# A float32 chain of decayed attention and two gated layers on one core: decay tables from prefix scans, first loads in another order, a new written order

## The chip, the cores and the metric

The kernel runs on one core of one Trainium2 chip. The metric is the device time of one execution in microseconds (us); the time given for a kernel is the median of its runs. A core has a matrix engine (TensorE, PE in the profile; PEld is its loading of weights), a vector engine (VectorE, DVE), an activation engine (ScalarE, ACT), a general engine (GpSimd, POOL) and a sync engine (SyncE, SP). Here SP issues most transfers (DMAs) and ACT a few. Every engine works through its own list of instructions in order; between engines they wait on semaphores.

## The reference

Three stages, all float32. `q`, `k`, `v` are 2 x 8 x 768 x 64 (batches, heads, tokens, channels), `lam` holds one decay factor a head, near 0.98.

```
intra = (q k^T * Dmask) v              # in a block; Dmask[i, j] = lam^(i-j) for i >= j, else 0
inter = (q * lam^(pos+1)) state        # what the blocks before left
state = lam^block * state + (k * lam^(block-1-pos))^T v
x  = attention output as 1536 x 512
xn = x / sqrt(mean(x*x) + 1e-6) * rms_g
x  = (silu(xn w_gate) * (xn w_val)) w_out      # 512 -> 1536 -> 512
x  = ((x w_a) * (x w_b)) w_out2                # 512 -> 1536 -> 512
```

## The kernel before, in words

Attention is cut into chunks of 128 tokens, six for each of the two batches. The weights arrive as 8-byte doubles and are turned into float32 on the chip: ACT copies two bytes of each (`conv_copy`, L275), DVE does the rest in seven steps (`conv_op`, L288 to L312). The two layers' matrix products take float32 operands split into a rounded high part (ACT, L325) and a low remainder (DVE, L330), three products a pair (L543, L544, L547, L599; L746 where the second layer and part of the first share block products).

The whole order of the program is written out by hand in `PROGRAM`, a list of words. A word is a step and its arguments; each step issues its instructions on its engines, and each engine keeps the order of the list. The words that matter here:

- `A.b.c.p`: SP loads two parts (or one) of batch b's chunk c, from part p on. Parts 0 and 1 are q and k by channels, 2 and 3 are v and k by tokens. `L.b.c` loads a whole later chunk. `l.n` loads the n-th third of the weights (512 KB, into one of three buffers `stage`).
- `S.b.c` scores (PE, L373, 16 passes), `am.b.c.r` the mask (DVE, L384): scores times the decay table `dt` for the even (r = 0) or odd heads. `X.b.c` masked scores times v (L423). `kd` decays k (ACT, eight small multiplications by the last column of `dt`, L366), `U` makes k^T v from it (L393), `I` is the inter-chunk product (L408) of q decayed by `qd` (DVE, L361, with the table `p1`, a part of `dec`).
- `xs`, `xd`: the attention output's high part (ACT, L456) and low part (DVE, L462, four instructions of 128 x 128). `sq`, `rh`, `rd`, `R`, `ms`: the mean square.
- `c.i.p` and `k.i.op.p` the conversion of weight block i, `hi.g.p` and `lo.g.p` its split, `G.g` and `V.g` the gate and value products (12 passes of 512 columns each on PE). `G.0` is the first of them and needs the attention output of chunks 0 and 1 of both batches.
- `W.n.1`: n dummy matmuls that nobody reads (`keep_warm`).

The tables are `dt`, 128 x 2 x 4 x 128 (for each head a triangle of powers), and `p1`, 128 x 4 x 128 (lam^(i+1)). Before the change they are made in three steps. DVE writes zeros, a one and the powers of `lam` into `ext` (8 rows of 256) by seven doublings (L858). ACT stores `ext` to DRAM (word `Z`). ACT then reads it back, each partition from an address shifted by one element (words `D.0` for `dt` and `D.1` for `p1`, two transfers each).

DMAs take eight completion semaphores in turn (`DMAHW0` to `DMAHW7`, SP's and ACT's together): where one is taken again, its issue waits until the transfer that had it has landed.

Of the kernel before, what the change touches and what calls it, by code (L numbers as in the profile page):

```python
# [44 lines left out]
def beside(i, t):  # L45
# [865 lines left out]
```

## Time and profile before

| | |
|---|---|
| time, median of 3 runs | 648.26 us (647.26 to 648.41) |
| time of the profiled execution | 647.11 us |
| its span, first to last instruction | 645.2 us |
| PE busy in the span | 626.1 us (97%) |
| DVE busy | 519.6 us (81%) |
| ACT busy | 374.4 us (58%) |
| POOL busy | 6.4 us (1%) |

The span is what the trace shows; 1.91 us of the execution lie around it. A busy share over the whole span says which engine is loaded, not what a stretch waits for; the rows further down take the span in stretches.

### The profile page before, as it was taken

To read this page: it belongs to the slowest core of one execution; us is meant where nothing else is said; L and a number is where in the kernel's file an instruction comes from. 1 tells how busy PE (TensorE), PEld (TensorE's weight loads), DVE (VectorE), ACT (ScalarE), POOL (GpSimd) and SP (SyncE) were. 2 spreads that over 40 slices of the span, in tenths; PEclk is the share of its full clock that TensorE was granted. 3 is DMA by queue.
4 is the path that set the end of the run, shared out by engine and by line. 5 is a ranking of instruction groups with operands and counts; after the bars stand their busy time and mean duration, and the time that the engine had idled before them with its cause. 6 is when DMAs were issued, how large, how long until landed. Compare 5 with 4: busy or idle time off the path is not lost.

```text
span 645.2 us, 8760 instructions
## 1 busy us (share of the span) xinstructions
PE 626.1 (97%) x3238; PEld 513.1 (80%) x3238; DVE 519.6 (81%) x965; ACT 374.4 (58%) x704; POOL 6.4 (1%) x15
## 2 busy tenths in 40 slices
PE   6689999999999999999999999999999999999997
PEld 3667888888888888888887888888888888888886
DVE  3678987888999889777989999999979854765673
ACT  2679877564558755455756655675567533443451
POOL 0000000000000000000000000000000000000000
PEclk8789999999999999999999999999999999999999
DMA  8826896432311230223002243121223000100011
GB/s 278 297 95 229 254 326 231 169 99 67 130 50 65 99 132 6 93 98 99 1 1 75 92 128 131 34 95 36 66 67 98 1 1 0 67 0 2 0 66 65
DMA packets 20394, 61.91 MB, mean 96 GB/s; under 512 B 2296, under 2 KB 3840, under 8 KB 19328
## 3 DMA queue, kind: packets, MB, share of 16 engines
q1 hardware_dynamic: 17872, 54.27, 25.2%
q10 hardware_dynamic: 2480, 7.09, 3.3%
q8 instruction: 25, 0.41, 0.3%
q14 instruction: 17, 0.14, 0.1%
HBM read 55.84 MB, written 5.51 MB: 95 GB/s over the span
## 4 chain that ended last, share of the span: by engine, by line
PE 92%; DVE 3%; DMA 2%; ACT 1%; issue 0%; ACTq 0%
PE acc L599 29%; PE at L746 17%; PE gv L746 13%; PE gv L543 6%; PE gv L544 6%; PE gv L547 6%; PE at L543 3%; PE at L544 3%; PE at L547 3%; PE at L373 2%; DMA dt<-ext_d 1%; PE at L408 1%; PE at L423 1%; DVE sums L611 1%; DMA ext_d<-nrm 1%; PE acc L423 1%
## 5 line engine op out<-in xcount | busy, mean ns | idle before, releaser
L275 ACT COPY hh<-stage 128x1024 uint8<-128x1024 uint8 x72 | 74.5, 1044 | 22.2 <-DMA stage<-w_dram 9.0
L325 ACT CAST whi<-w 128x512 fp32r<-128x512 f32 (+1 forms) x102 | 57.6, 576 | 30.0 <-PE acc L599 12.1
L543 PE MATMUL gv<-xhi,whi 128*128 128x512 f32 x160 | 64.6, 403 | 0.0
L544 PE MATMUL gv<-xlo,whi 128*128 128x512 f32 x160 | 63.2, 395 | 0.0
L330 DVE TENSOR_TENSOR wlo<-w,whi 128x512 fp32r<-128x512 f32 (+1 forms) x90 | 55.5, 622 | 8.8 <-ACT whi L325 8.7
L325 ACT CAST whi<-o 128x512 fp32r<-128x512 f32 x72 | 43.8, 620 | 18.0 <-PE acc L599 6.6
L330 DVE TENSOR_TENSOR wlo<-o,whi 128x512 fp32r<-128x512 f32 x66 | 44.9, 685 | 5.8 <-ACT whi L325 5.8
L746 PE MATMUL at<-T,whi 128*128 128x512 f32 x172 | 46.0, 389 | 0.0
L599 PE MATMUL acc<-hhi,whi 128*128 128x512 f32 x144 | 43.9, 395 | 0.1
L599 PE MATMUL acc<-hlo,whi 128*128 128x512 f32 x144 | 43.8, 390 | 0.0
L547 PE MATMUL gv<-xhi,wlo 128*128 128x512 f32 x160 | 43.2, 392 | 0.0
L599 PE MATMUL acc<-whi,hlo 128*128 128x512 f32 x144 | 43.0, 389 | 0.0
L599 PE MATMUL acc<-hhi,wlo 128*128 128x512 f32 x144 | 43.0, 390 | 0.0
L599 PE MATMUL acc<-whi,hhi 128*128 128x512 f32 x144 | 41.7, 390 | 0.0
L599 PE MATMUL acc<-wlo,hhi 128*128 128x512 f32 x144 | 41.4, 389 | 0.0
L330 DVE TENSOR_TENSOR wlo<-wsum,whi 128x512 fp32r<-128x512 f32 x42 | 28.8, 686 | 13.9 <-ACT whi L325 13.8
L746 PEld LDWEIGHTS at<-T,whi 128*128 128x128 f32 x172 | 32.2, 188 | 6.8 <-issue 0.2
L543 PEld LDWEIGHTS gv<-xhi,whi 128*128 128x128 f32 x160 | 30.3, 190 | 6.9 <-issue 0.5
L547 PEld LDWEIGHTS gv<-xhi,wlo 128*128 128x128 f32 x160 | 30.5, 190 | 6.5
L544 PEld LDWEIGHTS gv<-xlo,whi 128*128 128x128 f32 x160 | 30.5, 191 | 6.1 <-DVE xlo L527 0.2
L325 ACT CAST whi<-wsum 128x512 fp32r<-128x512 f32 x42 | 26.0, 621 | 13.5 <-DVE wsum L715 8.6
L746 PE MATMUL at<-xhi,whi 128*128 128x512 f32 x86 | 33.7, 391 | 0.0
(169 smaller groups left out, 1412.2 us busy)
## 6 DMA issues: line engine op xcount, KB each, us to landing
stage<-w_dram SPq DMA_DIRECT2D x72, 512.0 KB, 3.5
att<-att_dram ACTq DMA_DIRECT2D x6, 1024.0 KB, 6.3
wlo<-wlo_d SPq DMA_DIRECT2D x18, 256.0 KB, 3.7
att<-att_dram SPq DMA_DIRECT2D x6, 512.0 KB, 6.1
out_dram<-sums SPq DMA_DIRECT2D x12, 256.0 KB, 2.1
wlo_d<-wlo SPq DMA_DIRECT2D x9, 256.0 KB, 5.3
att<-att_dram SPq DMA_DIRECT2D x2, 1024.0 KB, 9.0
att<-att_dram SPq DMA_DIRECT2D x4, 256.0 KB, 6.9
```

Source lines behind the costliest of these rows:

```text
L275: nc.scalar.copy(hh_t[i][:, into].bitcast(U8).rearrange("p (n e) -> p n e", e=2), st.rearrange("p (n e) -> p n e", e=8)[:, :, 3:5],)
L325: nc.scalar.copy(whi[key], src)
L330: nc.vector.tensor_sub(wlo[key], src, whi[key].bitcast(F32))
L373: nc.tensor.matmul(ps[r][:, a * C : (a + 1) * C], lhsT=t[r * D : (r + 1) * D, 1, a * C : (a + 1) * C], rhs=t[r * D : (r + 1) * D, 0, a * C ...
L408: nc.tensor.matmul(px_t[b, c][r * D : (r + 1) * D, a * C : (a + 1) * C], lhsT=st_t[b][r * D : (r + 1) * D, a, :], rhs=kq_t[b, c][r * D : ( ...
L423: nc.tensor.matmul(px_t[b, c][r * D : (r + 1) * D, a * C : (a + 1) * C], lhsT=att_t[b, c][:, 2, h * D : (h + 1) * D], rhs=a_t[b, c][:, r, ...
L543: nc.tensor.matmul(ps, lhsT=w, rhs=xhi[t][:, k, :], start=k == 0, stop=False)
L544: nc.tensor.matmul(ps, lhsT=w, rhs=xlo[t][:, k, :], start=False, stop=False)
L547: nc.tensor.matmul(ps, lhsT=w, rhs=xhi[t][:, k, :], start=False, stop=k == KD - 1)
L599: nc.tensor.matmul(acc[j], lhsT=lhsT, rhs=rhs, start=first and n == 0, stop=last and n == 2)
L611: nc.vector.tensor_add(sums[t][:, j, :], sums[t][:, j, :], acc[j])
L746: nc.tensor.matmul(ps, lhsT=w[:, k * 128 : (k + 1) * 128], rhs=x[:, k, :], start=first and n == 0, stop=n == len(todo) - 1, skip_group_che ...
```

## The change

The tables no longer go by way of DRAM. `lam` is loaded into all 128 partitions at once (`lam_all`, 128 x 8). GpSimd writes an antidiagonal of ones (`anti`). VectorE makes each head's table with one prefix scan along 128 columns: eight scans for `dt`, four for `p1`. Word `D.r` is now the scans of the even or odd heads, `Z` those of `p1`. The seven doublings, the store and the four transfers back are gone; some constants are set by DVE instead of POOL.

```
-        nc.sync.dma_start(out=lam8, in_=lam)
+        nc.sync.dma_start(out=lam_all, in_=bass.AP(lam.tensor, lam.offset, [[0, 128], [1, H]]))
         nc.vector.memset(warm, 0.0)
-        nc.vector.memset(ext[:, 0:127], 0.0)
-        nc.vector.memset(ext[:, 127:128], 1.0)
-        nc.gpsimd.memset(ones, 1.0)
-        nc.gpsimd.memset(mhalf, -0.5)
-        nc.gpsimd.memset(ident, 1.0)
+        nc.vector.memset(mhalf, -0.5)
+        nc.vector.memset(ones, 1.0)
+        nc.vector.memset(ident, 1.0)
+        nc.gpsimd.affine_select(
+            out=anti, in_=ones, compare_op=ALU.is_equal, fill=0.0, base=1 - C,
+            pattern=[[1, 128]], channel_multiplier=1,
+        )
...
-        nc.vector.tensor_copy(ext[:, 128:129], lam8)
-        n = 1
-        while n < 128:
-            nc.vector.tensor_scalar_mul(
-                ext[:, 128 + n : 128 + 2 * n], ext[:, 128 : 128 + n], ext[:, 127 + n : 128 + n]
-            )
-            n *= 2
+        for r in range(2):
+            some = slice(r * D, (r + 1) * D)
+            nc.gpsimd.tensor_copy(lam_own[some], lam_all[some].rearrange("p (a r) -> p a r", r=2)[:, :, r])
...
+    def mask_table(r):
+
+        for a in range(NP):
+            h = 2 * a + r
+            nc.vector.tensor_tensor_scan(
+                out=dt[:, r, a, :], data0=lam_all[:, h : h + 1].to_broadcast([128, C]), data1=anti,
+                initial=0.0, op0=ALU.mult, op1=ALU.add,
+            )
+
+    def query_table():
+
+        for a in range(NP):
+            nc.vector.tensor_tensor_scan(
+                out=p1[:, a, :], data0=lam_own[:, a : a + 1].to_broadcast([128, C]), data1=ones,
+                initial=1.0, op0=ALU.mult, op1=ALU.mult,
+            )
```

`PROGRAM` is new from its first word up to word 992 of 2004; the words are the same ones, and from there on the order is the same. Its first line, before and now:

```
-    l.1 k.0.2.2 Z l.0 c.0.2 D.0 A.0.0.0 D.1 W.2.1 W.3.1 W.7.1 S.0.0 k.0.0.2 k.0.1.2 A.1.0.0 W.8.1 A.1.0.2 c.0.1 k.0.2.1
...
+    D.1 W.8.1 A.0.0.0 S.0.0 l.0 W.7.1 c.0.1 Z A.0.0.2 g D.0 am.0.0.1 A.1.0.0 k.0.0.1 am.0.0.0 l.1 k.0.1.1 X.0.0 kd.0.0
```

On DVE, at the start of the program, the difference of the two lists of instructions reads as follows (`-` before, `+` now; the scans print as SCALAR_TENSOR_TENSOR, `nrm` is the tile that holds `anti`, `w` a converted weight block, `am` a masked score).

```order
-L858 TENSOR_SCALAR nrm<-nrm 8x32
-L858 TENSOR_SCALAR nrm<-nrm 8x64
-L288 TENSOR_SCALAR w_122<-stage 128x512
+L847 MEMSET warm 128x256
+L848 MEMSET mhalf 128x2
+L849 MEMSET ones 128x128
+L850 MEMSET ident 128x128
+L795 SCALAR_TENSOR_TENSOR dt<-lam_all,nrm 128x128 x4
+L803 SCALAR_TENSOR_TENSOR dec<-lam_own,ones 128x128 x4
+L795 SCALAR_TENSOR_TENSOR dt<-lam_all,nrm 128x128 x4
+L384 TENSOR_TENSOR am<-at_129,dt 128x512
```

Twelve scans now stand ahead of the first mask, and the weight conversion that stood there comes after it.

On SP, the head of the queue before the change, with the semaphores that an issue waits for (`lam_84` is the factors, `att_0_131` batch 0's and `att_0_163` batch 1's chunk 0, `att_1` chunk 1, `g_sb` is `rms_g`):

```order
L843 DMA lam_84<-lam_dram 8x1
L249 DMA stage<-w_dram 128x4096 x2
L239 DMA att_0_131<-att_dram 128x1024
L239 DMA att_0_163<-att_dram 128x1024 x2
L239 DMA att_0_131<-att_dram 128x1024 [waits DMAHW2_49]
L239 DMA att_1_207<-att_dram 128x1024 [waits DMAHW4_49]
L239 DMA att_1_209<-att_dram 128x512 [waits DMAHW5_49]
L819 DMA g_sb<-gn_dram 128x4 [waits DMAHW6_49]
L239 DMA att_1_209<-att_dram 128x1024 [waits DMAHW7_49]
L239 DMA att_1_207<-att_dram 128x512 [waits DMAHW0_49]
L239 DMA att_1_207<-att_dram 128x512 [waits DMAHW1_49]
```

And now (`att_0_126` and `att_1_218` are batch 0, `att_0_161` and `att_1_229` batch 1):

```order
L846 DMA lam_all<-lam_dram 128x8
L239 DMA att_0_126<-att_dram 128x1024
L249 DMA stage<-w_dram 128x4096
L239 DMA att_0_126<-att_dram 128x1024
L822 DMA g_sb<-gn_dram 128x4
L239 DMA att_0_161<-att_dram 128x1024
L249 DMA stage<-w_dram 128x4096
L239 DMA att_0_161<-att_dram 128x1024
L239 DMA att_1_218<-att_dram 128x1024 [waits DMAHW0_49]
L239 DMA att_1_229<-att_dram 128x1024 [waits DMAHW1_49]
L239 DMA att_1_229<-att_dram 128x512 [waits DMAHW2_49]
L239 DMA att_1_218<-att_dram 128x512 [waits DMAHW3_49]
```

Batch 0's q and k are now the first large transfer, a weight load stands between the parts, and the eight semaphores are held by loads alone.

On ACT, the difference at the same place (`hh` are the copied bytes of the weights, `whi` a high part, `spare` and `kq` hold the decayed k):

```order
 L863 ACT_TABLE_LOAD
 L863 ACTIVATE mhalf<-mhalf 128x2
-L818 DMA ext_d<-nrm 8x256
-L275 COPY hh<-stage 128x1024
-L795 DMA dt<-ext_d 128x4x128 x2
-L800 DMA dec<-ext_d 64x4x128 x2
-L275 COPY hh<-stage 128x1024
-L325 CAST whi<-w_122 128x512
-L366 ACTIVATE spare<-att_0_163,dt 128x64 x8
-L366 ACTIVATE kq<-att_0_131,dt 128x64 x8
```

ACT's list loses the five issues of the tables' transfers; now the two rows at its head are followed by a weight copy and by the decay of batch 0's k.

## Rows read from the trace of the kernel before

**Rows 1.** Busy time by stretch: engines with instruction counts, granted clock, DMA share, GB/s.

```profile
core 0: us, PE busy (x) PEld busy (x) DVE busy (x) ACT busy (x) POOL busy (x), PEclk, DMA share, GB/s
0.00:17.34 17.34, 9.93 (x52) 4.91 (x52) 5.64 (x21) 4.17 (x6) 0.96 (x9) 0.90 0.85 269
17.34:41.40 24.06, 18.28 (x204) 16.00 (x205) 16.95 (x48) 16.23 (x52) 0.70 (x1) 0.79 0.67 233
41.40:86.70 45.30, 43.09 (x391) 35.97 (x390) 39.10 (x90) 39.65 (x109) 2.69 (x3) 0.96 0.70 229
86.70:360.00 273.30, 273.21 (x1356) 224.16 (x1357) 237.98 (x429) 167.33 (x295) 2.00 (x2) 1.00 0.29 96
360.00:645.20 285.20, 281.55 (x1240) 232.09 (x1238) 219.92 (x380) 146.97 (x247) 0.00 (x0) 1.00 0.16 52
```

**Rows 2.** The chain of waits, first microseconds: start, us, what.

```profile
0.79 1.32 DMA lam<-lam_dram
...
4.09 5.44 DMA ext_d<-nrm
...
10.03 8.59 DMA dt<-ext_d
```

**Rows 3.** Timeline of VectorE: start, us, operation, idle before and its releaser.

```profile
2.30 1.76 DVE L858 TENSOR_SCALAR nrm<-nrm 8x1 f32<-8x1 f32 x7
...
7.44 0.69 DVE L298 SCALAR_TENSOR_TENSOR w<-w,hh 128x512 f32<-128x512 uint32 x1
...
17.34 0.69 DVE L384 TENSOR_TENSOR am<-at,dt 128x512 f32<-128x512 f32 x1 [2.68 <-DMA dt<-ext_d]
```

**Rows 4.** Transfer queue of SP: who waited for whom, us in total, times, longest.

```profile
SPq L819 <- DMA dt<-ext_d: 6.9, 1, 6.9
```

**Rows 5.** Transfers: issue to landing of `g_sb` and `stage`; rates of two stretches.

```profile
g_sb<-gn_dram SPq DMA_DIRECT2D x1, 2.0 KB, 2.2
...
DMA to landing us min/median/max: 3.5/4.4/6.9
...
2.00:14.00 12.00, 9.17 (x51) 4.63 (x49) 4.65 (x16) 2.68 (x5) 0.10 (x1) 0.86 0.97 328
14.00:24.00 10.00, 5.29 (x52) 5.04 (x54) 5.86 (x13) 5.54 (x22) 0.00 (x0) 0.70 0.79 199
```

**Rows 6.** VectorE and GpSimd groups by shape: busy us, mean ns, idle before.

```profile
L384 DVE TENSOR_TENSOR am<-at,dt 128x512 f32<-128x512 f32 x8 | 5.4, 682 | 2.7 <-DMA dt<-ext_d 2.7
L462 DVE SCALAR_TENSOR_TENSOR xlo<-acc,g_sb,xhi 128x128 fp32r<-128x128 f32 x16 | 4.5, 344 | 3.4 <-ACT xhi L456 3.4
...
L288 DVE TENSOR_SCALAR w<-stage 128x512 uint32<-128x512 uint32 x6 | 2.5, 421 | 0.7 <-DMA stage<-w_dram 0.7
...
L305 DVE TENSOR_SCALAR t<-hh 128x512 uint16<-128x512 uint16 x5 | 1.4, 289 | 7.1 <-ACT hh L275 7.1
...
L494 POOL TENSOR_TENSOR rr<-ms,mhalf 128x2 f32<-128x2 f32 x6 | 5.4, 900 | 139.7 <-DVE ms L487 139.7
```

**Rows 7.** Timeline of TensorE: start, us, operation, idle before and its releaser.

```profile
8.21 2.08 PE L373 MATMUL at<-att 64*128 64x128 f32 x16 [2.47 <-DMA att<-att_dram]
10.22 2.36 PE L809 MATMUL gv<-warm 128*128 128x512 bf16 x8
...
20.58 0.44 PE L423 MATMUL acc<-am,att 128*64 128x128 f32 x1
...
31.32 1.68 PE L423 MATMUL acc<-am,att 128*64 128x128 f32 x16
...
41.40 0.47 PE L543 MATMUL gv<-xhi,whi 128*128 128x512 f32 x1
...
44.52 1.47 PE L547 MATMUL gv<-xhi,wlo 128*128 128x512 f32 x4
...
57.53 0.50 PE L543 MATMUL gv<-xhi,whi 128*128 128x512 f32 x1
...
59.48 1.07 PE L547 MATMUL gv<-xhi,wlo 128*128 128x512 f32 x4
```

More of the change, by code (lines that the diff above doesn't have):

```diff
@@ new lines @@
+    xs.0.0 sq.0.0 A.1.0.2 xd.0.0 S.1.0 U.0.0 A.0.1.0 c.0.2 kd.1.0 A.1.1.0 am.1.0.0 rh.0.0 W.3.1 am.1.0.1 k.0.2.1 rd.0.0
+    X.1.0 qd.0.1 R.0.0 sa.0.0 k.0.3.1 k.0.0.2 A.1.1.2 A.0.1.3 k.0.2.2 S.0.1 ms.0.0 A.0.1.2 U.1.0 l.4 qd.1.1 sq.1.0
+    xs.1.0 am.0.1.0 I.0.1 rh.1.0 am.0.1.1 S.1.1 xd.1.0 rd.1.0 am.1.1.0 kd.0.1 sa.1.0 sd.0.1 k.0.5.1 l.3 R.1.0 l.2 X.0.1
+    ms.1.0 c.1.1 k.0.1.2 am.1.1.1 U.0.1 sq.0.1 xs.0.1 k.1.2.1 I.1.1 X.1.1 rr.0 k.0.3.2 dg.0 rh.0.1 k.0.5.2 xs.1.1
+    A.1.1.3 L.0.2 N.0 rv.0 rd.0.1 k.0.6.1 xd.0.1 R.0.1 xd.1.1 c.1.0 sq.1.1 k.1.2.0 rh.1.1 ms.0.1 hi.0.0 rd.1.1 W.2.1
@@ new lines @@
+    kd.1.1 l.5 S.0.2 kd.0.2 k.1.0.0 R.1.1 L.1.2 lo.0.0 am.0.2.1 ms.1.1 k.1.1.0 qd.0.2 rr.1 dg.1 sa.0.1 G.0 N.1 rv.1
+    c.1.2 qd.1.2 am.0.2.0 k.2.2.0 k.1.0.1 k.1.3.0 k.1.0.2 I.0.2 X.0.2 sd.0.2 k.0.6.2 sq.0.2 xg.0.2 k.1.1.1 l.8 U.0.2
+    k.1.2.2 sa.0.2 k.1.1.2 rh.0.2 hi.0.1 L.0.3 k.1.3.2 U.1.1 S.1.2 k.1.3.1 lo.0.1 V.0 l.7 k.1.5.0 rd.0.2 k.1.5.1
+    am.1.2.1 ls.0.0 kd.1.2 sd.1.1 R.0.2 am.1.2.0 k.1.6.1 sa.1.1 c.2.0 U.1.2 ms.0.2 hi.1.0 gs.0 k.2.2.2 ls.0.1 l.6 I.1.2
+    si.0 X.1.2 qd.0.3 sd.1.2 lo.1.0 k.1.5.2 sq.1.2 mu.0 xg.1.2 k.1.6.2 sa.1.2 c.2.2 G.1 rh.1.2 c.2.1 hh.0 rd.1.2 R.1.2
@@ new lines @@
+    k.1.6.0 ms.1.2 hi.0.2 L.0.4 k.2.0 hi.1.1 kd.0.3 hl.0 S.0.3 am.0.3.1 I.0.3 rr.2 sd.0.3 am.0.3.0 l.9 k.2.1 hi.3.0
+    dg.2 k.2.3 lo.1.1 X.0.3 U.0.3 k.2.5 L.1.3 sq.0.3 k.2.2.1 xg.0.3 V.1 k.2.6 lo.0.2 N.2 nx.2.0 nx.2.2 O.0 rh.0.3
+    nx.2.1 l.10 nx.2.3 ls.1.0 rd.0.3 sa.0.3 hi.1.2 k.3.2.0 c.3.1 R.0.3 c.3.0 ms.0.3 qd.1.3 hi.2.0 l.11 S.1.3 hi.2.1
+    c.3.2 am.1.3.1 am.1.3.0 gs.1 I.1.3 k.3.2.1 kd.1.3 X.1.3 U.1.3 si.1 xg.1.3 l.12 lo.2.0 G.2 lo.1.2 sq.1.3 ls.1.1
+    k.3.2.2 rh.1.3 mu.1 rd.1.3 hi.4.0 hi.3.1 qd.0.4 lo.2.1 ls.2.0 l.13 ls.2.1 sd.1.3 R.1.3 hh.1 ms.1.3 rr.3 V.2 k.3.0
@@ new lines @@
+    gs.2 lr.4.0 xh.2.0 sa.1.3 kd.0.4 dg.3 hl.1 xl.2.0 N.3 L.1.4 lr.3.0 nx.3.3 O.1 hi.5.0 k.3.1 si.2 nx.3.0 nx.3.2
+    xh.2.1 xh.3.1 nx.3.1 xl.2.1 S.0.4 xl.3.1 xh.3.0 c.4.2 c.4.1 xl.3.0 lr.3.1 mu.2 c.4.0 k.3.3 am.0.4.1 hi.4.1 ls.0.2
+    G.3 ls.1.2 k.3.5 k.4.2.1 am.0.4.0 k.3.6 I.0.4 sd.0.4 U.0.4 si.3 X.0.4 sa.0.4 sq.0.4 hi.4.2 hh.2 l.16 V.3 k.4.2.0
+    hl.2 mu.3 hi.2.2 xg.0.4 kd.1.4 lo.2.2 c.5.2 rh.0.4 rd.0.4 S.1.4 G.4 hi.9.0 hh.3 hi.5.1 k.4.2.2 am.1.4.1 l.15 lr.5.0
+    lo.9.0 O.2 L.0.5 R.0.4 qd.1.4 lr.4.1 si.4 am.1.4.0 k.4.0 ms.0.4 V.4 c.5.1 I.1.4 k.5.2.2 lr.5.1 k.4.1 sd.1.4 E.2.0
@@ new lines @@
+    G.10 am.1.5.1 xh.4.0 lr.6.2 xl.4.1 gs.10 O.5 hi.7.1 rd.0.5 am.1.5.0 hh.9 k.6.3 k.6.5 l.22 R.0.5 k.6.6 G.11 V.10
+    ms.0.5 hl.9 k.8.2.0 hi.12.0 lr.7.2 c.7.2 gs.11 c.8.0 I.1.5 E.5.1 si.10 lo.12.0 mu.10 lo.9.2 X.1.5 E.5.3 hi.12.1
+    k.7.0.0 sq.1.5 E.5.0 rh.1.5 xg.1.5 G.12 E.5.2 lo.12.1 rd.1.5 k.7.2.0 xl.4.0 k.7.1.0 hh.10 R.1.5 ms.1.5 hi.11.1 rr.5
+    O.9 dg.5 si.11 lo.11.1 hi.10.2 hl.10 N.5 k.7.3.0 lo.10.2 k.7.5.0 l.24 nx.5.2 l.21 nx.5.0 nx.5.1 k.7.6.0 c.7.1 V.11
+    gs.12 mu.11 hh.11 nx.5.3 hi.6.1 xh.5.0 O.10 hl.11 hi.7.0 xh.5.1 lr.7.0 c.8.1 xl.5.0 k.7.0.2 tq.3.0 xl.5.1 tq.3.1
@@ new lines @@
+    k.7.3.1 P.3.5 ws.4.1 pa.3.1 ws.3.4 uh.3.2 P.3.6 ws.4.2 k.7.5.1 hi.7.2 P.4.2 ul.3.2 ps.3.6 P.3.7 hh.8 k.7.6.1 ps.3.5
+    hl.8 uh.4.1 l.28 k.8.2.2 sl.3.1 hi.8.2 k.8.0 l.26 ws.4.3 ws.4.4 P.3.3 pa.3.3 k.7.6.2 uh.4.2 ps.4.1 O.7 ps.3.7
+    ul.4.2 ul.3.3 ul.4.1 P.3.4 ws.5.3 pm.3.1 c.9.2 ws.5.1 uh.5.3 ph.3.1 lr.8.2 k.9.2.2 l.31 uh.5.0 pa.3.2 ws.5.2
+    k.9.2.1 P.4.5 k.9.2.0 uh.3.4 ps.4.5 O.8 k.8.1 E.8.0 pa.4.1 P.4.6 ul.5.0 uh.5.1 sl.3.2 k.8.3 pm.3.2 c.9.1 k.8.5
+    pl.3.1 ps.4.6 P.5.2 E.8.2 P.5.1 E.8.3 l.29 ps.5.1 ws.5.4 c.9.0 uh.4.3 ul.3.4 ul.5.1 P.4.3 pa.4.3 ws.6.1 P.4.7
@@ new lines @@
+    uh.4.4 ul.5.3 ul.4.4 ul.4.3 sl.4.1 P.5.6 l.30 ps.4.7 P.4.4 E.8.1 k.8.6 pa.5.1 P.5.5 uh.6.0 k.9.0 sl.4.2 Q.3.1.0.9
+    uh.5.2 ul.5.2 pa.4.2 Q.3.1.9.12 ws.6.2 ps.5.5 pm.4.1 sl.5.1 ps.5.6 ul.6.0 P.5.3 c.10.0 ph.4.1 pm.4.2 P.5.7 k.9.1
+    P.6.2 k.9.3 ws.6.4 c.10.1 pl.4.1 ps.5.7 P.6.1 c.10.2 Q.4.1.0.9 uh.6.1 Q.4.1.9.12 ws.6.3 pa.5.3 k.10.2.2 ps.6.1
+    k.9.5 k.10.0 hi.13.0 uh.5.4 ul.6.1 pa.6.1 k.9.6 sl.6.1 P.6.6 sl.5.2 k.10.2.0 ws.7.1 hi.14.1 uh.6.2 l.34 ps.6.6
+    k.10.2.1 P.6.5 P.5.4 k.10.1 lo.14.1 pm.5.1 ul.5.4 pa.5.2 ul.6.2 V.14 uh.6.3 pm.5.2 ps.6.5 k.11.2.2 k.10.3 P.6.7
@@ new lines @@
+    ph.5.1 P.6.3 ul.6.3 ps.6.7 lo.13.0 uh.3.5 hi.14.0 P.6.4 pl.5.1 pa.6.3 pm.6.1 ph.6.1 c.11.2 hi.15.0 Q.5.1.0.9 uh.6.5
+    l.32 k.10.5 Q.5.1.9.12 l.33 lo.14.0 pa.6.2 pl.6.1 k.10.6 ph.3.2 uh.6.4 G.13 ul.6.4 G.14 l.37 c.12.2 Q.6.1.0.9
+    c.11.0 k.11.2.0 gs.13 sl.6.2 uh.4.5 lo.15.0 Q.6.1.9.12 ws.7.2 hi.16.0 G.15 e.6.1.2 ph.4.2 l.40 e.6.1.0 e.6.1.1
+    k.11.2.1 k.12.2.2 c.11.1 hi.13.1 pl.4.2 ul.3.5 lo.13.1 e.6.1.3 k.11.0 si.13 pl.3.2 k.11.1 V.13 l.36 uh.8.0 k.12.2.1
+    uh.7.1 gs.14 ul.6.5 l.35 c.12.1 lo.16.0 ul.4.5 l.39 Q.3.2.0.12 k.11.3 k.11.5 ul.7.1 uh.5.5 si.14 ul.5.5 Q.4.2.0.12
@@ L114 @@
+    hh.17 ps.7.5 O.16 k.14.2.0 hi.17.2 l.42 ws.8.3 c.14.0 ps.7.1 P.8.1 ws.8.4 l.45 P.7.6 ul.7.3 P.7.3 c.14.1 ps.7.6
+    pa.7.1 k.14.2.1 uh.9.0 lo.17.2 uh.7.4 pa.7.3 P.7.7 hl.17 ul.7.4 ps.7.7 sl.7.1 O.17 c.13.0 pa.7.2 sl.7.2 uh.8.2
+    uh.8.1 ps.8.1 P.7.4 E.17.1 E.17.2 ul.8.1 pm.7.1 E.17.0 P.8.2 uh.8.3 l.43 ul.8.2 l.44 ph.7.1 P.8.5 ps.8.5 c.14.2
     k.14.2.2 pl.7.1 E.17.3 pm.7.2 P.8.6 ul.8.3 l.46 ul.9.0 P.8.3 ws.9.1 ps.8.6 pa.8.1 ws.9.2 Q.7.1.0.9 uh.9.1 pa.8.3
@@ L201, in bank @@
         return psum.tile([128, 512], F32, tag=tag, name=tag)
-    lam8 = cpool.tile([H, 1], F32, tag="lam8", name="lam8")
+    lam_all = cpool.tile([128, H], F32, tag="lam_all", name="lam_all")
+    lam_own = cpool.tile([128, NP], F32, tag="lam_own", name="lam_own")
     nrm = tpool.tile([128, 512], F32, tag="nrm", name="nrm")
-    ext = nrm[0:H, 0:256]
+    anti = nrm[:, 256:384]
     am = tpool.tile([128, B, 2, 512], F32, tag="am", name="am")
@@ L788, in pair_out @@
         out_part(i, (i, "u", 3 + t), h_t[i, t], first, last, slice(a, b))
-    def decay_tables(q):
-        for r in range(2):
-            if q == 0:
-                nc.scalar.dma_start(
-                    out=dt[:, r],
-                    in_=bass.AP(ext_d.tensor, ext_d.offset + r * 256, [[1, 128], [512, NP], [1, C]]),
-                )
-            else:
-                nc.scalar.dma_start(
-                    out=p1[r * D : (r + 1) * D],
-                    in_=bass.AP(ext_d.tensor, ext_d.offset + r * 256 + 128, [[0, D], [512, NP], [1, C]]),
-                )
+    def mask_table(r):
[11 more added lines that the diff above has]
+            )
     def keep_warm(n, where=0):
@@ L817, in chain_kernel @@
         "l": load_w, "A": load_first, "L": lambda b, c: load_att(b, c, queue=nc.sync if c == 2 else nc.scalar),
-        "Z": lambda: nc.scalar.dma_start(out=ext_d, in_=ext), "D": decay_tables,
+        "D": mask_table, "Z": query_table,
         "g": lambda: nc.sync.dma_start(out=g_sb, in_=gn),
```

75 lines of the change are left out of this document (15 added, 60 removed).

## The prediction

> **What bounds the kernel now.** I read the stretch table first [rows 1]. The reader is to see that TensorE is the bound of nearly all of the span: from 86.70 us on it is busy 273.21 of 273.30 us and then 281.55 of 285.20. Nothing that comes earlier on another engine helps there; what helps is that TensorE gets to that state sooner. Ahead of it stand 17.34 us in which VectorE works 5.64, then 24.06 us in which no engine is over 76% busy, then 45.30 us in which VectorE has 39.10 and TensorE 43.09. So the change is worth what it takes from the first 87 us, less what it puts back.
>
> The chain of waits shows why the first 17 us are slow [rows 2]: `lam` lands, the powers are built, `ext` goes out (5.44 us), the tables come back (8.59 us). VectorE's timeline shows the end of it: the first mask starts at 17.34, released by the transfer of `dt`, after 2.68 us idle [rows 3]. The scores had long been there: the first `S` ran at 8.21 [rows 7]. The same transfers also hold up the loads: the issue of `g_sb`, and the chunk-1 loads behind it on SP, waited 6.9 us for `dt`, whose semaphore it takes over [rows 4]. The first gate product, `G.0`, starts at 41.40 [rows 7].
>
> **The change part by part.** *First mask.* The new `lam_all` is issued first, at 0.79 as `lam` was [rows 2]. It has 128 rows where `lam` had 8, so I take the 2.2 us of `g_sb`, which has 128 rows too, [rows 5] rather than `lam`'s 1.32: it lands at 2.99 (bounds 2.11 and 2.99). DVE's four constants and POOL's select of `anti` lie beside that flight. POOL's two copies for `lam_own` lie beside the first four scans; at the 0.90 us of POOL's costliest row [rows 6] they would end at 4.8 against 4.4 for the scans, so they cost 0.4 at worst, and I take nothing.
>
> No scan is in the trace. The nearest row is the instruction of the same size and class, 128 x 128 with three operands: 344 ns [rows 6]. A scan's step needs the one before it, so I take the whole duration with no overlap: 12 x 0.344 = 4.1 us, first mask at 7.1. Bounds: 0.28 us, where they overlap as those rows do (16 of them are 4.5 us of busy time), hence 3.4 us in all; and the 0.682 us of a 512-column row [rows 6], 8.2 us in all and the first mask at 11.2. The scores are ready in time: the first load is now q and k, 512 KB, and such a transfer at the head took 3.5 us to land [rows 5], so about 1.2 + 3.5 = 4.7, plus 2.08 for `S.0.0` [rows 7], 6.8. The seven dummies behind it take 7/8 of 2.36 us [rows 7], to 8.9; the second mask, one conversion step of 0.29 and one mask more of 0.68 [rows 6] later, ends at 8.8. `X.0.0` thus starts at 8.9 where the first L423 stood at 20.58 [rows 7], 11.7 sooner; the first mask is 17.34 - 7.1 = 10.2 sooner. I take the smaller, **10.2**.
>
> [...] No run here shows a scan yet.
>
> *The loads.* Up to the last part that `X.0.1` needs there are 4.98 MB on SP (eight loads of 512 KB, three of 256). At the 328 GB/s of the stretch from 2 to 14 us [rows 5] and with about 3 us of start and latency they are in at 18.2. `X.0.1` stood at 31.32 [rows 7]; 10.2 sooner is 21.1, so the loads are hidden by 2.9 us. Of the weights `l.0` stays second among the large loads, and `l.1` goes from first to fifth, to 3 + 5 x 0.52 MB / 0.328 = 11; what covers that is that only `V.0` wants it, after `G.0`. ACT loses five issues and their waits; its list behind them (the weight copy, the first `kd`) moves up with the tables.
>
> *From the first mask to `G.0`.* This took 24.06 us with VectorE busy 16.95 [rows 1]. Now the conversions that stood ahead of the first mask lie in it: two steps of 0.42, six of 0.29 [rows 6], one of 0.43 and one of 0.69 [rows 3], together 3.7 us. On the other side the new order leaves some of VectorE's words for after `G.0`: out go `k.0.6.2` (0.69), `lo.0.1` and `am.0.2.0` (0.68 each), `k.1.2.2` (0.42) and four steps of 0.29; in come `qd.0.2` (0.68), `sa.0.1` and `k.1.2.0` (0.42 each) and two of 0.29. That is 3.63 out, 2.10 in, 1.5 less. Net 2.2 us more in a stretch where it idles 7.1, waiting for ACT and TensorE. I let half of it show: **-1.1** (0 to -2.2). What waits behind: `xd.0.0` waits on ACT's `xs.0.0`, and behind it on VectorE the two masks of batch 1, for which `X.1.0` waits; that wait existed before.
>
> *From `G.0` to 86.7.* The 1.5 us come back here, and the new list has three more words ahead of `G.3`, the product at 86.7: `mu.2`, `am.0.4.1` (0.68 each) and a step of about 0.55. That is 3.4 us more for an engine with 6.2 idle in 45.30 [rows 1], while TensorE idles 2.2. Half of it: **-1.7** (0 to -3.4). VectorE is what is late next.
>
> *Clock.* TensorE was granted 0.79 of full speed, mixed from its two levels, in the second stretch [rows 1]. `G.0` took from 41.40 to 45.99, 4.6 us, the like product at 57.53 3.0 us [rows 7]. A better fed start could give 1.6 us back; I take none. The dummies are 20 as before.
>
> Sum: 10.2 - 1.1 - 1.7 = 7.4 us. The span goes from 645.2 to 637.8, with 1.91 us around it 639.7. The profiled execution lies 1.15 below the median of the runs shown, so by the median **640.9**. Its own range, with the bounds of the two stretches, is a gain of 4.6 to 10.2: 638.1 to 643.7.
>
> **Rivals.** *The lead is kept whole, and the clock helps.* VectorE's idle 7.1 and 6.2 us take all its extra work, and `G.0` runs at full clock: 10.2 to 11.8 us gained, 636.5 to 638.1. For it: X's own lead of 11.7. Against: VectorE is at 86% from `G.0` on.
>
> *The loads bind instead.* If the full queue moves only the 199 GB/s of 14 to 24 us [rows 5], 4.98 MB are in at 28, 7 us after `X.0.1` wants them: only about 3 us gained, 645.2. Against: SP's queue was blocked in that stretch.
>
> *The new order opens gaps later.* Between 86.7 and 360, TensorE has nothing to gain and VectorE 35 us of slack; a wait that the new list puts there could take back anything from half to all, 645 to 648.
>
> *The scans are slow, and it gets slower.* The trace's own way of building powers serially, seven dependent steps on small tiles, takes 1.76 us [rows 3] for one set. If a scan costs that, twelve are 21.1 us, the first mask comes at 24.1, 6.8 late, and with the 1.1 us of the second stretch the time is 656. It decides from (17.34 - 2.99) / 12 = 1.2 us a scan. Against: VectorE streams every other row of this class at about 1 to 3 ns a column.
>
> **How the numbers follow.** The forecast gets 0.65, the whole lead 0.15, binding loads 0.07, later gaps 0.06, slow scans 0.05, other slow outcomes 0.02. 0.2% is 1.3 us, about what a measurement of this kernel can tell from no change. Faster: 0.65 + 0.15 and 0.08 of the two small-gain rivals, 0.88; the same: 0.05; slower: 0.07. The range runs from the whole lead, 636.5, to the case of loads that bind with a little over it, 645.5; gains over 11.8 and under 2.8 are left out, with about 0.15.
>
> **What would show it.** In the new profile: twelve scans of 0.28 to 0.68 us from about 3 us on; first mask near 7, `X.0.0` near 9, `G.0` near 32, `G.3` near 79; VectorE over 90% busy from 32 to 79, and TensorE without a gap from there to its old tail. Wrong if a scan is over 1 us, if SP's loads of chunk 1 land after 21, if TensorE's waits between `G.0` and `G.3` on VectorE are over 4 us, or if it waits after `G.3` at all.

## The result and the profile after

The changed kernel takes 639.64 us (median of 4 runs, 639.41 to 639.80), the kernel before 648.34 in the same rounds: a ratio of 0.9866, interval 0.9849 to 0.9883, 8.7 us faster. The forecast was 640.9 in 636.5 to 645.5, a gain of 7.4. The profiled execution has a span of 637.9 us where the forecast had 637.8: 7.3 of the 8.7 us are in the spans of the two profiled executions, most of the rest is that the one of before (647.11 us) was shorter than any of its other runs.

The stretch table of the changed kernel, divided at the first mask, `G.0` and `G.3` as [rows 1], and then so that the last row has the 285.2 us that it has there, with the same columns:

```profile
0.00:8.80 8.80, 5.71 (x25) 2.93 (x26) 4.46 (x16) 2.35 (x3) 1.23 (x9) 1.00 0.73 209
8.80:30.30 21.50, 17.61 (x233) 13.46 (x232) 17.57 (x54) 18.26 (x60) 1.23 (x1) 1.00 0.96 346
30.30:78.80 48.50, 44.39 (x391) 36.79 (x390) 40.94 (x95) 39.24 (x103) 2.95 (x3) 0.93 0.65 223
78.80:352.70 273.90, 273.81 (x1359) 224.43 (x1358) 238.15 (x428) 168.63 (x296) 1.56 (x2) 1.00 0.29 95
352.70:637.90 285.20, 281.34 (x1239) 232.02 (x1237) 219.84 (x380) 147.10 (x247) 0.00 (x0) 1.00 0.16 52
```

The reader is to compare lengths. The first stretch went from 17.34 to 8.80 (8.5 us won), the second from 24.06 to 21.50 (2.6 won), the third from 45.30 to 48.50 (3.2 lost), the fourth from 273.30 to 273.90 (0.6 lost). The last has its length by this choice, but matched rows say the same: TensorE's first L543 product after 360 us stood at 360.58 and its counterpart now at 353.12, 7.46 us sooner, and the last product of all at 641.16 and 633.66, 7.50 sooner (the two lists are the same from word 1001 on). The granted clock rose from 0.79 to 1.00 in the second stretch and fell from 0.96 to 0.93 in the third. The 1.00 of the first row is no reading: the trace has no clock record before 9.72 us, and time without a record counts as full in this column. `S.0.0` took 2.08 us there, as it did at the lower level before [rows 7], where the next scores, at 11.82, took 1.16.

VectorE's timeline at the start, against [rows 3]:

```profile
3.51 1.37 DVE L795 TENSOR_TENSOR_SCAN dt<-lam_all,nrm 128x128 f32<-128x128 f32 x4 [2.03 <-DMA lam_all<-lam_dram]
4.79 1.34 DVE L803 TENSOR_TENSOR_SCAN dec<-lam_own,ones 128x128 f32<-128x128 f32 x4
6.06 1.35 DVE L795 TENSOR_TENSOR_SCAN dt<-lam_all,nrm 128x128 f32<-128x128 f32 x4
8.81 0.69 DVE L384 TENSOR_TENSOR am<-at,dt 128x512 f32<-128x512 f32 x1 [1.40 <-PE at L373]
```

The twelve scans take 3.9 us, from 3.51 to 7.41. But the mask then waits 1.40 us for TensorE's scores: the tables are no longer what is late. TensorE's timeline says why, and shows what happens later (against [rows 7]):

```profile
6.68 2.08 PE L373 MATMUL at<-att 64*128 64x128 f32 x16 [1.85 <-DMA att<-att_dram]
...
11.82 1.16 PE L373 MATMUL gv<-att 64*128 64x128 f32 x16
...
30.29 0.48 PE L543 MATMUL gv<-xhi,whi 128*128 128x512 f32 x1
...
50.02 2.11 PE L373 MATMUL at<-att 64*128 64x128 f32 x16
52.92 1.97 PE L408 MATMUL at<-kq,st 64*64 64x128 f32 x16 [0.78 <-DVE am L384]
54.82 1.97 PE L423 MATMUL at<-am,att 128*64 128x128 f32 x16
```

q and k were issued at 1.22 and are used at 6.68, 5.4 us later and not 3.5. `G.0` starts at 30.29 against 41.40, a lead of 11.1 us. At 50 us `S.0.3`, `I.0.3` and `X.0.3` take about twice the 1.09 us that the latter two take elsewhere. The waits of VectorE and TensorE in that part, and the clock:

```profile
DVE kq L361 <- DMA att<-att_dram: 2.7, 1, 2.7
```

```profile
PE at L482 <- DVE sq L477: 1.4, 1, 1.4
```

```profile
48.00:50.00 2.00, 0.57 (x4) 1.00 0.62 229
50.00:52.00 2.00, 2.00 (x17) 0.67 0.37 66
52.00:54.00 2.00, 1.22 (x11) 0.50 0.98 414
54.00:56.00 2.00, 2.00 (x22) 0.50 0.15 53
56.00:58.00 2.00, 2.00 (x26) 0.62 0.16 25
```

(The last fence is the stretch table for TensorE alone: its busy time, clock, DMA share, GB/s.) `qd.0.3` waits on VectorE for chunk 3, issued at 37.04 and landed at 45.75. Everything behind it on VectorE comes 2.7 us late, TensorE runs dry for 1.4 us before 50, and then its clock is at the lower level (0.50) for some 7 us (by the trace's records from 50.69 to 57.51). A table of milestones in the profiled executions, read from the timelines, carries this through all kernels that follow (us; medians of the runs at the right):

| kernel | first mask | `G.0` | `V.1` | `G.3` | span | median |
|---|---|---|---|---|---|---|
| before | 17.34 | 41.40 | 65.37 | 86.62 | 645.2 | 648.3 |
| changed | 8.81 | 30.29 | 57.58 | 78.79 | 637.9 | 639.6 |
| tables only | 12.51 | 35.41 | 58.12 | 79.36 | 638.3 | 640.0 |
| order only | 20.28 | 41.86 | 67.75 | 89.44 | 648.2 | 650.1 |
| weights first | 10.43 | 32.44 | 57.68 | 81.03 | 639.9 | 641.3 |
| scans twice | 11.12 | 33.06 | 60.28 | 81.58 | 640.5 | 642.2 |
| `lam` second | 10.40 | 32.28 | 59.53 | 80.92 | 640.1 | 640.8 |
| no dummies | 9.00 | 30.89 | 53.98 | 75.19 | 634.1 | 639.2 |
| `qd.0.3` later | 8.85 | 31.84 | 54.13 | 75.36 | 634.2 | 636.6 |
| that, and `lam` as a row | 7.15 | 28.85 | 50.92 | 72.13 | 631.1 | 634.5 |

Medians of different batches stand on different chips; the kernel before had 648.3, 646.0, 648.6 and 647.5 in the four. What is compared closely below was run side by side.

### The profile page after: what moved, and what is told of

Read it like the earlier page. It is cut to its first block, busy times and chain, and to the rows that moved or that the text cites. A ratio compares the mean times of both kernels' runs of the same rounds, so it can differ in the third digit from the quotient of the medians.

```text
span 637.9 us, 8754 instructions
## 1 busy us (share of the span) xinstructions
PE 622.9 (98%) x3238; PEld 509.6 (80%) x3238; DVE 521.0 (82%) x970; ACT 375.6 (59%) x704; POOL 7.0 (1%) x15
## 4 chain that ended last, share of the span: by engine, by line
PE 91%; DVE 5%; DMA 2%; ACT 1%; issue 0%; POOL 0%; SPq 0%; ACTq 0%; POOLq 0%
PE acc L599 29%; PE at L746 18%; PE gv L746 13%; PE gv L543 6%; PE gv L544 5%; PE gv L547 5%; PE at L544 3%; PE at L543 3%; PE at L547 3%; DMA att<-att_dram 2%; PE at L373 2%; PE at L408 1%; PE at L423 1%; DVE sums L611 1%; DVE xlo L462 1%; DVE am L384 1%
## 5 line engine op out<-in xcount | busy, mean ns | idle before, releaser
L543 PE MATMUL gv<-xhi,whi 128*128 128x512 f32 x160 | 64.3, 402 | 0.0
L763 ACT COPY usum<-at 128x512 f32<-128x512 f32 x32 | 18.8, 587 | 29.2 <-PE at L746 23.7
L543 PEld LDWEIGHTS gv<-xhi,whi 128*128 128x128 f32 x160 | 30.0, 188 | 7.4 <-issue 0.5
```

The lines of the kernel that those rows point to most:

```text
L543: nc.tensor.matmul(ps, lhsT=w, rhs=xhi[t][:, k, :], start=k == 0, stop=False)
L763: nc.scalar.copy(block("u")[:, n == 7], (px if n == 7 else pd)[i])
```

## The experiments

**Which part of the change is worth what.** Two kernels each do one half. The first has the scans with the written order of before:

```
-PROGRAM = (the new list)
+PROGRAM = (the list of before, unchanged)
```

> The scans and the new constants with the written order of before, so weights first on SP and the weight conversion ahead of the first mask on VectorE. Theory (the tables' way through DRAM was what held the start, and order and loads each add a part): twelve scans run behind the first conversion step from about 5.3 to 9.2 us, seven conversion steps and three more follow, first mask near 13 instead of 17.3, chunk-1 loads no longer held on SP; 3 to 5 us gained, 643.5 to 645.5 us. Rival 1 (the tables alone are the whole gain): 639 to 641. Rival 2 (the order alone is the gain, the tables only allow it): 647 to 649.

The second has the new order with the tables of before, so the list begins:

```
-    D.1 W.8.1 A.0.0.0 S.0.0 l.0 W.7.1 c.0.1 Z A.0.0.2 g D.0 am.0.0.1
+    Z D.0 D.1 W.8.1 A.0.0.0 S.0.0 l.0 W.7.1 c.0.1 A.0.0.2 g am.0.0.1
```

> The written order of the change with the tables of before (powers by doublings, stored to DRAM and read back by ACT; the three words that make them stand first, since a store has to stand ahead of its reads). Theory: the first mask stays near 17 to 18 us, VectorE has no conversion ahead of it to fill the wait, so 3.7 us of conversion fall behind it: 0 to 4 us slower than before, 648 to 652. Rival (the new order is good by itself): 642 to 646.

Measured: tables only 640.04 us, ratio to before 0.9897 (0.9877 to 0.9918); order only 650.11, ratio 1.0053 (1.0035 to 1.0071). My theory for the first was wrong: not 3 to 5 us, but 6.0 against before in the same batch (646.03), and the time that rival 1 gave, that of the whole change. VectorE's timeline of the kernel with the tables only:

```profile
5.61 1.36 DVE L803 TENSOR_TENSOR_SCAN dec<-lam_own,ones 128x128 f32<-128x128 f32 x4
6.89 2.60 DVE L795 TENSOR_TENSOR_SCAN dt<-lam_all,nrm 128x128 f32<-128x128 f32 x8
12.51 0.68 DVE L384 TENSOR_TENSOR am<-at,dt 128x512 f32<-128x512 f32 x1
```

The first mask came as expected, near 13, and `G.0` at 35.41 is 5.1 us behind the changed kernel. But from there on it makes this good: `V.1` is 0.5 us behind, the span 0.4. The order alone is slower, as expected, though the first mask came at 20.28 and not near 17 to 18. Its timeline shows the tables late and TensorE's long wait:

```profile
20.28 0.69 DVE L384 TENSOR_TENSOR am<-at,dt 128x512 f32<-128x512 f32 x1 [16.21 <-DMA dt<-ext_d]
```

```profile
PE acc L423 <- DVE am L384: 13.3, 1, 13.3
```

To rule out that two chips made the two kernels look alike, tables only and the changed kernel ran again beside each other, five rounds:

> The changed kernel unchanged, as the measure for the three beside it on the same chip: 637.5 to 640 us.

> The tables alone, with the written order of before, beside the changed kernel on one chip. Theory (at the end the new order and the loads are worth nothing, since the 5 us by which they lead at the first gate product are lost again before V.1): within 1.3 us of the changed kernel. Rival (the two fell together by the difference between chips): 2 us or more slower.

Changed 639.65 (ratio 0.9888, 0.9867 to 0.9908), tables only 640.55 (0.9903, 0.9882 to 0.9925): 0.9 us apart with intervals that overlap, within the 1.3 us of the expectation. The profiles of this batch are less alike: tables only is 6.1 us behind at `G.0`, 3.4 at `V.1` and 3.3 in the span, but its profiled execution, 642.53 us, was the slowest of its six. So what is left of the 5 us at the end rests on the medians, not on single profiles.

**What a microsecond at the first mask is worth.** Two ways to delay it: the loads as before, and twice the scans.

```
-    D.1 W.8.1 A.0.0.0 S.0.0 l.0 W.7.1 c.0.1 ... am.0.0.0 l.1 k.0.1.1
+    D.1 l.1 l.0 W.8.1 A.0.0.0 S.0.0 W.7.1 c.0.1 ... am.0.0.0 k.0.1.1
```

> The changed kernel with two weight loads of 512 KB ahead of the first q and k on SP, as before the change. Theory (the first mask waits for the scores, these for the load of q and k): q and k land 2.5 to 3.5 us later, first mask near 11.5 to 12, and most of that reaches the end: 641.5 to 643. Rival (VectorE's work from the first mask to the first gate product is the bound and the weights, now earlier, help it): within 0.7 us of 639.6. If the first transfer behind lam_all again takes over 5 us to land although it is a weight load, the factors' load of 128 short rows slows what follows it; if it lands in 3.5 to 4, the q and k load itself is slow.

```
-    D.1 W.8.1 ... c.0.1 Z A.0.0.2 g D.0 am.0.0.1
+    D.1 D.1 W.8.1 ... c.0.1 Z Z A.0.0.2 g D.0 D.0 am.0.0.1
```

> The changed kernel with each of the twelve scans done twice (same tables). 3.9 us more of VectorE ahead of the first mask, of which 1.4 were idle. Theory (first mask to first gate product is one rigid chain): first mask near 11.3, the end 2 to 3 us later, 641.6 to 642.6. Rival (slack of VectorE behind takes it): within 0.7 us of 639.6.

Weights first 641.33, scans twice 642.19. First the timelines of VectorE, weights first and scans twice:

```profile
10.43 0.69 DVE L384 TENSOR_TENSOR am<-at,dt 128x512 f32<-128x512 f32 x1 [2.90 <-PE at L373]
```

```profile
3.52 2.63 DVE L795 TENSOR_TENSOR_SCAN dt<-lam_all,nrm 128x128 f32<-128x128 f32 x8 [2.05 <-DMA lam_all<-lam_dram]
...
11.12 0.66 DVE L384 TENSOR_TENSOR am<-at,dt 128x512 f32<-128x512 f32 x1
```

Against the changed kernel the first mask is 1.6 and 2.3 us later, `G.0` 2.2 and 2.8, the span 2.0 and 2.6. In these profiles a delay there goes through to the end whole, and VectorE's slack behind takes none of it. The medians agree in sign, 1.7 and 2.6 us over the changed kernel's 639.64, but come from another chip, where the kernel before ran 2.3 us faster. The kernel of the next experiment was run beside the changed one: first mask 1.6 us later, 2.1 later in the median, with intervals that overlap. The load of q and k at the head of SP is worth 1.6 to 2 us (q and k landed 1.6 us later; I had expected 2.5 to 3.5), and the scans' 3.9 us have 1.4 us of cover.

**Why q and k land late.** One kernel issues them ahead of the factors:

```
+        load_first(0, 0, 0)
         nc.sync.dma_start(out=lam_all, ...)
...
-    D.1 W.8.1 A.0.0.0 S.0.0 l.0
+    W.8.1 S.0.0 D.1 l.0
```

> The changed kernel with the first load of q and k issued ahead of the load of the decay factors. If the factors' load with its 128 short rows slows the transfers behind it, q and k land 3.5 to 4.5 us after their issue instead of 5.4, at about 4.5 to 5.3 us, and the scans start later, at 4 to 5 us: first mask 0 to 1 us sooner, end 638.6 to 639.6. Rival (the q and k load is slow by itself, or by the loads issued right behind it): it takes over 5 us again and the scans start 0.5 to 3 us later, end 639.6 to 641.

Timelines of VectorE and of TensorE in this kernel:

```profile
6.59 1.37 DVE L795 TENSOR_TENSOR_SCAN dt<-lam_all,nrm 128x128 f32<-128x128 f32 x4 [5.11 <-DMA lam_all<-lam_dram]
```

```profile
4.91 1.25 PE L373 MATMUL at<-att 64*128 64x128 f32 x16
```

Issued at 0.79, q and k were there by 4.91 (behind the dummies, with no wait), at most 4.1 us: about 1.3 us less than behind the factors. With the one row per head of before ahead of them (order only) they landed 4.4 us after their issue. So the load of 128 short rows delays what follows it by about 1 us, as the first theory said. It is not the whole delay. In the kernel with the weights first, a weight load of the same 512 KB stood right behind the factors, and by the test set for that run it says the other half:

```profile
DMA to landing us min/median/max: 4.0/4.5/4.9
```

The line is for its first two weight loads; the first, issued at 1.21, landed at 5.26. So behind the 128 rows weights took 4.0 us where q and k took 5.4, and behind the 8 rows of before weights took 3.5 [rows 5] where q and k took 4.4 (order only). The kind of load is worth 1.0 to 1.4 us, the factors' 128 rows 0.6 to 1.0. Why q and k take longer than weights of the same size stays open. In the kernel with `lam` second, though, the factors landed at 6.5, 5.3 us after issue, and the scans came 3.1 us later and not 0.5 to 1.5: the rival's end, 640.82 against 638.76 for the changed kernel in that batch:

> The changed kernel once more, unchanged, on the chip of the three kernels beside it, so that they can be compared with it directly: 638.5 to 640.5 us.

**The clock.** All 20 dummies taken out of the list (they compute nothing that is read):

```
-    W.8.1 ... W.7.1 ... W.3.1 ... W.2.1
```

> The changed kernel without the 20 dummy matmuls that only keep TensorE busy. Theory (the full clock that the changed kernel is granted in its first 50 us comes from denser work of TensorE, dummies among it, and is worth part of the lead at G.0): half clock shows in the records between 5 and 30 us, G.0 comes at 31 to 33 instead of 30.3, and the end is 0.5 to 2 us later. Rival (the start is bound by VectorE and ACT, not by the clock): same within 0.7 us.

The lower level did show, the loss did not: 639.17 us against 638.76 for the changed kernel in that batch, within the rival's 0.7, with four times from 635.80 to 641.36. TensorE's timeline (this kernel's line numbers are one less):

```profile
6.87 2.08 PE L372 MATMUL at<-att 64*128 64x128 f32 x16 [6.87 <-DMA att<-att_dram]
10.54 1.97 PE L422 MATMUL acc<-am,att 128*64 128x128 f32 x16 [1.59 <-DVE am L383]
12.44 2.08 PE L372 MATMUL gv<-att 64*128 64x128 f32 x16
...
18.26 1.16 PE L372 MATMUL at<-att 64*128 64x128 f32 x16
```

TensorE had no work up to 6.87 us. Its scores took 2.08 us at 6.87 and at 12.44, and 1.16 at 18.26: it ran at the lower level up to about 14.6 us, where the first clock record of this trace starts (at full). The clock column reads 1.00 before that, too, for want of a record. So the rise comes some 5 us later than in the changed kernel, and yet `G.0`, at 30.89, is only 0.6 us later.

With the dummies a late rise costs more. Five executions have the same list up to `G.0`: three of the changed kernel and the two with the moved word below. Their first clock records, at full, start at 9.65, 9.72, 10.27, 10.59 and 12.99 us, and their `G.0` at 30.23, 30.29, 30.54, 30.71 and 31.84, about half a microsecond for each microsecond of later rise. What sets the time of the rise was not found.

The span of the execution without dummies is 3.8 us shorter than the changed kernel's, and 3.6 of that stand at `V.1`. There the wait for chunk 3 was 1.3 us and not 2.7, TensorE's wait for `sq` 0.8 and not 1.4, and the clock did not fall; in all three profiles of the changed kernel it fell after such a wait of 1.4 us. So the fall goes with the wait here; one execution cannot say that nothing else matters. Runs of one kernel in one batch differ by 0.2 to 5.6 us, as much as these effects.

**Where the new order's lead goes.** One word is moved behind seven words of VectorE that do not need chunk 3 (the expectation counts nine):

```
-    si.0 X.1.2 qd.0.3 sd.1.2 lo.1.0 ... rh.1.2 ... rd.1.2 R.1.2
+    si.0 X.1.2 sd.1.2 lo.1.0 ... rh.1.2 ... rd.1.2 qd.0.3 R.1.2
```

> The changed kernel with one word moved: qd.0.3, which waits on VectorE for the load of chunk 3 and stood ahead of the low part of block 1, now stands nine words of VectorE later, after rd.1.2. Theory (this wait of 2.7 us starves TensorE before S.0.3, its clock falls to half, and both together eat the 5 us by which the new order leads at G.0): no wait there, full clock from 50 to 57 us, V.1 near 53 instead of 57.6, 3 to 5 us gained, 635 to 637. Rival (another wait takes its place, since chunk 3 lands at 45.8 whatever is done): within 1 us of 639.6.

> The moved word once more, beside the changed kernel. Theory (the wait on VectorE for chunk 3 is where the new order's lead is lost): 2 to 4 us faster than the changed kernel, with full clock from 50 to 57 us. Rival (noise of single runs): within 1 us of it.

636.61 (ratio 0.9828, 0.9797 to 0.9858) against 638.76 (0.9858, 0.9826 to 0.9889) in one batch; 637.32 (0.9847, 0.9821 to 0.9873) against 639.65 in the other: 2.2 and 2.3 us faster twice, under the 3 to 5 us of the first expectation and at the low end of the second's 2 to 4, with intervals that overlap. VectorE and TensorE's clock in the first one's profile:

```profile
47.65 0.68 DVE L361 TENSOR_TENSOR kq<-att,dec 128x512 f32<-128x512 f32 x1
```

```profile
50.00:52.00 2.00, 0.98 (x16) 1.00 1.06 401
...
54.00:56.00 2.00, 2.00 (x16) 1.00 0.40 74
```

No wait, full clock, `V.1` at 54.13. TensorE still waits 1.0 us there for a mask. The second one's profile had the wait for chunk 3 gone too, but TensorE waited 1.8 us for the same mask, the clock was at the lower level from 51.2 to 54.6, and `V.1` came at 55.21: the wait is cured by the move, the clock only in part.

**A version that beats both.** The moved word, and the factors loaded as one row:

```
-        nc.sync.dma_start(out=lam_all, in_=bass.AP(lam.tensor, lam.offset, [[0, 128], [1, H]]))
+        nc.sync.dma_start(out=lam_row, in_=bass.AP(lam.tensor, lam.offset, [[H, 1], [1, H]]))
...
+        keep_warm(2, 1)
+        spread_lam = bank("at0")[:, 0:H]
+        nc.tensor.matmul(spread_lam, lhsT=ones[0:1, :], rhs=lam_row, start=True, stop=True)
+        nc.vector.tensor_copy(lam_all, spread_lam)
...
-    D.1 W.8.1 A.0.0.0
+    D.1 W.6.1 A.0.0.0
```

> The moved word, and the decay factors loaded as one row of eight, spread to the 128 partitions by one matmul with ones and one copy of VectorE instead of a load of 128 short rows. Theory (that load lands late, at 3.5, and holds up the q and k load behind it by about 1 us): scans start near 2.8 and q and k land near 5.6, first mask 1 to 1.5 us sooner, end 0.5 to 1.5 us before the kernel with the moved word alone. Rival (from the first mask on VectorE and ACT give the pace, or q and k land late anyway): same within 0.5 us.

634.48 us, ratio 0.9811 (0.9785 to 0.9836), against 637.32 with the moved word alone and 639.65 for the changed kernel: 2.8 us sooner than the moved word alone, where 0.5 to 1.5 were expected, with intervals that overlap a little. Its timelines, VectorE and TensorE:

```profile
2.83 0.17 DVE L855 COPY lam_all<-at 128x8 f32<-128x8 f32 x1 [1.36 <-PE at L854]
3.11 1.37 DVE L796 TENSOR_TENSOR_SCAN dt<-lam_all,nrm 128x128 f32<-128x128 f32 x4
...
7.15 0.69 DVE L385 TENSOR_TENSOR am<-at,dt 128x512 f32<-128x512 f32 x1
```

```profile
2.20 0.59 PE L854 MATMUL at<-lam_row,ones 1*128 1x8 f32 x2
...
5.95 1.16 PE L374 MATMUL at<-att 64*128 64x128 f32 x16 [0.48 <-DMA att<-att_dram]
```

Against the changed kernel the scans start 0.4 us sooner, q and k are used 0.7 sooner, the scores run in 1.16 us and not 2.08, and the first mask is 1.7 us sooner. So 0.9 of the 1.7 us is the clock, at full from 5.85 us on here, and whether the one-row load brought that is not shown. `G.0` is 1.4 sooner than in the changed kernel, in line with the delays above. The rest of the gain lies after `G.0`, where this profile shows full clock throughout, and is within the spread of single runs.

## Why the prediction was right, and where its steps were off

*What bounds, and why only the first 87 us matter:* right. Of the 7.8 us won at `G.3`, 7.3 are in the span.

*The sum, 7.4 us:* that the spans show 7.3 is luck. Its terms were off by -1.7 (first mask), +3.7 (to `G.0`) and -1.5 (to `G.3`), about 0.5 went behind `G.3`, and they cancel.

*First mask, 10.2 us:* 8.5. The scans' sum came out, 3.9 us where 4.1 stood, by two errors: one takes 0.402 us and not 0.344, and they overlap, 0.32 us from one to the next, where I took none. VectorE's groups by shape show the price of a column:

```profile
L361 DVE TENSOR_TENSOR kq<-att,dec 128x512 f32<-128x512 f32 x4 | 2.8, 689 | 2.7 <-DMA att<-att_dram 2.7
L473 DVE TENSOR_TENSOR sq<-sq 128x256 f32<-128x256 f32 x8 | 3.4, 422 | 1.0 <-ACT sq L469 1.0
L477 DVE TENSOR_TENSOR sq<-sq 128x128 f32<-128x128 f32 x8 | 2.3, 290 | 0.0
L795 DVE TENSOR_TENSOR_SCAN dt<-lam_all,nrm 128x128 f32<-128x128 f32 x8 | 2.7, 402 | 2.0 <-DMA lam_all<-lam_dram 2.0
```

Rows of two operands take 290, 422 and 689 ns for 128, 256 and 512 columns, 1.04 ns a column on top of 157. With that 157 the scan's 402 leave 1.9 ns a column, nearly twice (an estimate: scans of one width alone were run).

The mis-sized term is the landing of q and k: "such a transfer at the head took 3.5 us to land", and it took 5.4; the scores, which I had ready in time, were what the mask waited for. The 3.5 us were those of a weight load behind 8 short rows. The factors' 128 rows ahead account for 0.6 to 1.0 us of the difference and the kind of load for 1.0 to 1.4, whose cause stays open. `lam_all` itself landed at 3.4, past my bound of 2.99.

*First mask to `G.0`, -1.1:* this had the wrong sign, +2.6. I let the extra VectorE work show by half; it all fitted. VectorE is busy 17.57 of 21.50 us where it was 16.95 of 24.06, so the waits for ACT and TensorE shrank from 7.1 to 3.9 us. The clock, left out of the sum, was at full for nearly all of this stretch (by the record from 9.72 us on), where it had been at 0.79. Other traces separate it from the list. Two kernels with the new list, order only and scans twice, had part of the stretch at the lower level:

```profile
20.28:41.86 21.58, 17.44 (x225) 14.40 (x226) 17.55 (x54) 17.70 (x58) 1.22 (x1) 0.87 0.69 224
11.12:33.06 21.94, 17.92 (x225) 14.63 (x226) 17.51 (x55) 17.17 (x56) 1.22 (x1) 0.84 0.84 299
```

They took 21.6 and 21.9 us. Of the eleven profiles with the new list or with a few words of it changed, ten took 21.4 to 22.0, and one, the first of the moved word, whose clock rose late, 23.0. The three with the list of before took 22.9 to 24.1. So most of the 2.6 us belongs to the new list.

*`G.0` to `G.3`, -1.7:* -3.2, nearly the bound of -3.4. The cause named was VectorE's extra work. What the runs show is one wait in it, `qd.0.3` for chunk 3, and the lower clock after TensorE ran dry: with the word moved, `G.3` came 3.8 and 1.7 us sooner than in the changed kernel's profile of the same batch. "VectorE is what is late next" was right only by way of a transfer that I had not looked at: my check of the loads ended with chunk 1. VectorE itself was busy 40.94 of 48.50 us, 84% and not the over 90% that was to be its sign.

*Rivals.* Binding loads did not come true for chunk 1: the last part that `X.0.1` needs landed at 17.4 (18.2 in the forecast), TensorE waited for no load of it, and SP's queue waited 0.9 us at most for landings ([rows 4] had 6.9). One part of chunk 1, `A.1.1.3`, did land after the 21 us of the sign, at 25.2, where the list has it behind three weight loads; no engine waited for it. The whole lead came true at `G.0` (11.1), and 3.3 us of it were lost before `G.3`. Slow scans and later gaps did not.

*What I credited wrongly:* the sum took tables, loads and order as one lead. By the experiments the tables alone bring 6.0 to 7.0 us in their batches; loads and order bring 5.1 us more up to `G.0` and end with 0.9 us or nothing. The order puts a wait at chunk 3, and moving that one word gives 2.2 to 2.3 us back.

## What to carry to other kernels

When a start-up step gets faster, look at once at who is late next and at the transfer behind that one, as far as the bound engine has no slack: here three parts gave a lead of 11 us, and a single in-order wait, with the lower clock behind it, took 2 to 3 back. Before thanking a new order for a gain, run the old order with the other part alone. And a tiny load is not free at the head of a queue: its shape and place can cost the big one behind it (here 0.6 to 1.0 us). Read a clock column together with the times of like instructions: a stretch without a record reads as full clock, as the first 9.72 us of the changed kernel did.

## What the runs showed of the hardware

A load of 128 rows of 32 bytes from one address took 2.6 to 2.9 us to land when it was first and 5.3 behind one 512 KB load; a load of one row of 32 bytes with a matmul of two passes (0.59 us) and a copy (0.17 us) had the same values in all partitions by 3.0 us. A 512 KB load behind those 128 rows took 4.0 us (weights) or 5.4 (q and k), behind 8 rows of 4 bytes 3.5 or 4.4, and q and k with nothing ahead at most 4.1. A prefix scan with a multiplication and an addition runs at 0.32 us per 128 columns, back to back. In the execution that had no work for TensorE up to 6.87 us, its products took the times of the lower level from there up to about 14.6 us. At 50 us its clock fell after 1.4 us without work in the three profiles of the changed kernel and after 1.8 in one of the moved word, and stayed full after 1.0 in the other and 0.8 without dummies; what decides the times of its rises and falls was not found.
